# Keeping a weight tile in the array for two sequence blocks: blocks 2 and 3 of the first matmul share each w1 tile

## The chip, the cores and the metric

One core of one Trainium2 chip. The time is the device time of one execution in microseconds; a median over runs is quoted with its range. Most executions of one kernel agree within 0.3%. Every comparison below is between runs in the fast state (a mean granted clock of the tensor engine of at least 0.988 of full speed); the one execution that was not is told of and used for nothing. The experiments ran on four chips, each beside the kernel before on the same chip, and every ratio is to that.

## The reference

```python
B, S, D, F = 1, 2048, 576, 4608          # all bfloat16
def reference(x, w1, b1, w2, b2):
    h = jnp.einsum("bsd,df->bsf", x, w1) + b1
    r = jnp.where(h > 0, h, 0)
    h = r * r                             # squared ReLU
    return jnp.einsum("bsf,fd->bsd", h, w2) + b2
```

## The kernel before

The sequence is cut into four blocks of 512 rows. D = 576 is nine times 64, so the first matmul contracts over 64 rows at a time, and two such matmuls run side by side in the upper and the lower half of the array ("row tiles"). A pair below means two such matmuls, one in each row tile, each streaming 512 columns. The kernel has three parts on the tensor engine:

1. The first matmul, block after block: per block 18 steps; a step makes two tiles of the hidden layer (one per row tile) in two PSUM banks, from 9 pairs. (The first two steps of block 0 are done otherwise while the first inputs arrive, so 70 steps, or 630 pairs, are counted below.) ScalarE then takes each bank out with ReLU and bias, and VectorE squares it.
2. The "64-column part": the last 64 columns of the output, for two blocks at a time, with 128x64 weights from w2.
3. The second matmul proper: per 128 output rows, 36 matmuls of 512 columns with 128x128 weights.

```python
    def a_part(b, j, bk, steps):
        for i in steps:
            for h in range(2):                       # h: upper or lower row tile
                c = ORDER[h][i]
                rows = slice(h * H, (h + 1) * H)
                nc.tensor.matmul(bk[h][:], lhsT=w1h[rows, c, j * P:(j + 1) * P], rhs=xT[b][rows, place(h, c), :],
                                 start=(i == 0), stop=(i == NH - 1))

    def a_step(b, j):
        bk = [bank("ph") for _ in range(2)]          # 8 banks in all, in turn
        a_part(b, j, bk, range(NH))
        for h in range(2):
            evac_h(b, pairs[j][h], bk[h])            # ScalarE: ReLU + bias; VectorE: square
    # ... cut ...
    load_w2(0)
    for b in range(1, NSB):
        for j in (*range(2, NJ), 0, 1):
            a_step(b, j)
            if j == NJ // 2 and b + 1 < NSB:
                finish_xT(b + 1)
        if b == 1:
            load_w2(1)
        if b == 2:
            load_w2(2, 2)                            # the memory of blocks 1 and 2 is free now
    # ... cut ...
    for pr in range(NSB // 2):                       # the 64-column part
        pc = bank("pc")
        for ft in range(NFT):
            for h in range(2):
                nc.tensor.matmul(pc[h * H:(h + 1) * H, :], lhsT=w2(ft, DM, D), rhs=hT_of(2 * pr + h, ft),
                                 start=(ft == 0), stop=(ft == NFT - 1))
        # ... cut: ScalarE adds b2, and a DMA transposes ...
```

Every matmul instruction is compiled into a weight load and a matmul. The transposed x of blocks 0 to 2 lies in memory that w2 takes over later, so a piece of w2 can be loaded only when the block that lay there has been used.

## Time and profile before

| | |
|---|---|
| time, median of the first 3 runs | 290.27 us (290.25 to 290.72) |
| span in the profile | 288.7 us |
| tensor engine (PE) busy | 284.9 us, 99% |
| weight loads (PEld) busy | 133.7 us, 46% |
| chain of waits | 98% PE |

The first two parts of the page: busy time with its share of the span and the number of instructions, and the busy tenths in 40 equal slices. PE is the tensor engine's matmuls, PEld its weight loads, DVE VectorE, ACT ScalarE, POOL GpSimd. PEclk is the granted clock in tenths of full speed (9 is 90% or more).

```profile
PE 284.9 (99%) x2067; PEld 133.7 (46%) x2078; DVE 79.5 (28%) x196; ACT 95.6 (33%) x153; POOL 1.5 (1%) x8
...
PEld 5544444444444444444445444444444444444454
...
PEclk9999999999999999999999999999999999999999
```

A busy PE says little of its pace, because matmuls are pipelined: each is recorded as 376 ns long, and several overlap. The pace is read from the chain of waits in order of time (start, length, what; `ph`, `pc` and `po` are the PSUM tiles of the three parts, and "issue" is time in which PE waited for nothing that the profile shows):

```profile
9.78 135.97 PE ph L213 x1260
145.75 15.66 PE pc L315 x144
161.41 0.32 PE po L329
...
285.97 0.29 DVE o_sb L331
```

The first matmul's 1260 matmuls are 630 pairs in 135.97 us, 215.8 ns a pair. The Trainium skill, "TensorE: Matmul & The Clock Gate", Part 2 (Step-by-step, phases on the wall clock), gives 512 columns at 2.4 GHz as 213 ns plus a fixed 2.5 ns or so, measured at 215.7 ns. This trace agrees.

The groups of instructions (line, engine, operation, shapes, count; busy us and mean ns of one; idle time before them and what ended it):

```profile
L213 PE MATMUL ph<-w_sb,w1h 64*128 64x512 bf16 x936 | 101.2, 376 | 0.0
L213 PEld LDWEIGHTS <-w1h 64*128 64x128 bf16 x1260 | 61.3, 94 | 74.6
...
L213 PE MATMUL ph<-xT,w1h 64*128 64x512 bf16 x324 | 35.1, 376 | 0.0
```

The last column of the matmul lines is 0.0 us of idle time before them. The load line has 74.6 us of idle time, which costs nothing, since loads are not what the others wait for. (How the busy time divides among two groups that overlap is arbitrary.)

### The profile page before, as it was taken

To read this page: it belongs to the slowest core of one execution; us is meant where nothing else is said; L and a number is where in the kernel's file an instruction comes from. 1 tells how busy PE (TensorE), PEld (TensorE's weight loads), DVE (VectorE), ACT (ScalarE), POOL (GpSimd) and SP (SyncE) were. 2 spreads that over 40 slices of the span, in tenths; PEclk is the share of its full clock that TensorE was granted. 3 is DMA by queue.
4 is the path that set the end of the run, shared out by engine and by line. 5 is a ranking of instruction groups with operands and counts; after the bars stand their busy time and mean duration, and the time that the engine had idled before them with its cause. 6 is when DMAs were issued, how large, how long until landed. Compare 5 with 4: busy or idle time off the path is not lost.

```text
span 288.7 us, 4818 instructions
## 1 busy us (share of the span) xinstructions
PE 284.9 (99%) x2067; PEld 133.7 (46%) x2078; DVE 79.5 (28%) x196; ACT 95.6 (33%) x153; POOL 1.5 (1%) x8
## 2 busy tenths in 40 slices
PE   9999999999999999999999999999999999999996
PEld 5544444444444444444445444444444444444454
DVE  1644454444445444444420011111100111111111
ACT  3666666766666676666620000000000000000000
POOL 2000000000000000000000000000000000000000
PEclk9999999999999999999999999999999999999999
DMA  7999999910400004300000100000000000000000
GB/s 200 205 190 204 172 185 208 321 50 2 122 3 0 3 2 142 106 0 2 0 2 19 20 20 20 20 23 5 15 20 23 20 20 20 23 20 22 20 23 20
DMA packets 35381, 18.01 MB, mean 62 GB/s; under 512 B 21652, under 2 KB 35360, under 8 KB 35360
## 3 DMA queue, kind: packets, MB, share of 16 engines
q1 hardware_dynamic: 34752, 17.14, 26.4%
q10 hardware_dynamic: 576, 0.56, 0.6%
q8 instruction: 16, 0.26, 0.4%
q14 instruction: 5, 0.04, 0.0%
q0 software_dynamic: 32, 0.01, 0.0%
HBM read 11.94 MB, written 2.36 MB: 50 GB/s over the span
## 4 chain that ended last, share of the span: by engine, by line
PE 98%; DMA 1%; issue 0%; DVE 0%; ACTq 0%
PE ph L213 47%; PE po L329 43%; PE pc L315 5%; PE ph L228 2%; DMA w_sb<-in_x_dram 1%; PE tp L182 1%; PE ph L254 0%; DVE o_sb L331 0%; PE b1T_ps L247 0%; ACTq L353 0%
## 5 line engine op out<-in xcount | busy, mean ns | idle before, releaser
L197 ACT ACTIVATE r<-ph,b1T 128x512 bf16<-128x512 f32 x144 | 91.0, 685 | 48.4 <-PE ph L213 46.4
L213 PE MATMUL ph<-w_sb,w1h 64*128 64x512 bf16 x936 | 101.2, 376 | 0.0
L213 PEld LDWEIGHTS <-w1h 64*128 64x128 bf16 x1260 | 61.3, 94 | 74.6
L329 PE MATMUL po<-w_sb,hT 128*128 128x512 bf16 x423 | 92.9, 379 | 0.5
L329 PEld LDWEIGHTS <-hT 128*128 128x128 bf16 x432 | 42.2, 98 | 51.2 <-issue 0.4
L199 DVE TENSOR_TENSOR hT<-r 128x512 bf16<-128x512 bf16 x108 | 46.0, 426 | 54.7 <-ACT r L197 54.2
L331 DVE TENSOR_TENSOR o_sb<-po,b_bc 128x512 bf16<-128x512 f32 (+2 forms) x17 | 11.2, 660 | 116.7 <-PE po L329 109.7
L213 PE MATMUL ph<-xT,w1h 64*128 64x512 bf16 x324 | 35.1, 376 | 0.0
L329 PE MATMUL po<-w_sb,w1h 128*128 128x512 bf16 (+2 forms) x178 | 31.2, 336 | 0.1
L329 PEld LDWEIGHTS <-w1h 128*128 128x128 bf16 x180 | 16.2, 98 | 15.3
L199 DVE TENSOR_TENSOR w1h<-r 128x512 bf16<-128x512 bf16 x36 | 15.3, 426 | 19.6 <-ACT r L197 19.5
L315 PE MATMUL pc<-hT,w_sb 128*64 128x512 bf16 x108 | 15.7, 379 | 0.0
L315 PEld LDWEIGHTS <-w_sb 128*64 128x64 bf16 x144 | 8.1, 110 | 7.6 <-issue 0.4
L315 PE MATMUL pc<-w1h,w_sb 128*64 128x512 bf16 x36 | 7.9, 379 | 0.0
L317 ACT ACTIVATE oc<-pc,b2T 128x512 bf16<-128x512 f32 x2 | 1.4, 687 | 13.7 <-PE pc L315 13.7
L325 DVE COPY o_sb<-oc 128x64 bf16<-128x64 bf16 x16 | 2.8, 172 | 9.3 <-DMA oc<-oc 9.3
L228 PE MATMUL ph<-w_sb 128*128 128x256 bf16 x32 | 5.3, 313 | 0.0
L228 PEld LDWEIGHTS <-w_sb 128*128 128x128 bf16 x32 | 3.4, 115 | 0.6
L175 DVE COPY w_sb<-tp 128x256 bf16<-128x256 bf16 x5 | 1.5, 292 | 5.9 <-PE tp L182 5.9
L182 PE MATMUL tp<-ident,w_sb 128*128 128x128 bf16 x20 | 2.7, 264 | 0.1
L169 PE MATMUL wps<-one 128*128 128x512 bf16 x5 | 2.3, 628 | 0.4 <-DVE one L144 0.4
L182 PEld LDWEIGHTS <-w_sb 128*128 128x128 bf16 x20 | 1.9, 118 | 1.4 <-DMA w_sb<-in_x_dram 1.2
(27 smaller groups left out, 10.7 us busy)
## 6 DMA issues: line engine op xcount, KB each, us to landing
w_sb<-in_w_dram SPq DMA_DIRECT2D x2, 1728.0 KB, 8.7
w1h<-in_w_dram SPq DMA_DIRECT2D x8, 288.0 KB, 5.9
out_dram<-o_sb SPq DMA_DIRECT2D x15, 144.0 KB, 1.8
w1h<-in_w_dram SPq DMA_DIRECT2D x12, 144.0 KB, 3.7
w_sb<-in_w_dram SPq DMA_DIRECT2D x2, 864.0 KB, 7.2
w1h<-in_w_dram SPq DMA_DIRECT2D x2, 576.0 KB, 11.2
w_sb<-in_x_dram SPq DMA_DIRECT2D x2, 144.0 KB, 3.4
w_sb<-in_x_dram ACTq DMA_DIRECT2D x2, 144.0 KB, 3.5
```

The lines of the kernel that those rows point to most:

```text
L169: nc.tensor.matmul(wps[:], lhsT=ones[:, 0:P], rhs=ones[:], start=(i == 0), stop=(i == NWARM - 1))
L175: nc.vector.tensor_copy(out=dst, in_=src)
L182: nc.tensor.transpose(tp[:, i * P:(i + 1) * P], xs[:, 2 * half + i, d0:d0 + P], ident[:])
L197: nc.scalar.activation(out=r[:], in_=bk[:], func=ACT.Relu, bias=b1T[:, ft:ft + 1], scale=1.0)
L199: nc.vector.tensor_tensor(out=hT_of(b, ft), in0=r3, in1=r3, op=ALU.mult)
L213: nc.tensor.matmul(bk[h][:], lhsT=w1h[rows, c, j * P:(j + 1) * P], rhs=xT[b][rows, place(h, c), :], start=(i == 0), stop=(i == NH - 1))
L228: nc.tensor.matmul(bk0[q][:, cols], lhsT=qn[:, c, q * P:(q + 1) * P], rhs=xT[0][:, c, cols], start=(half == 0 and c == 0), stop=False, ski ...
L315: nc.tensor.matmul(pc[h * H:(h + 1) * H, :], lhsT=w2(ft, DM, D), rhs=hT_of(2 * pr + h, ft), start=(ft == 0), stop=(ft == NFT - 1))
L317: nc.scalar.activation(out=oc[:, pr, :], in_=pc[:], func=ACT.Identity, bias=b2T[:], scale=1.0)
L325: nc.vector.tensor_copy(out=o_sb[:, DM:D], in_=o_tr[pr][:, jj, h * H:(h + 1) * H])
L329: nc.tensor.matmul(po[:, 0:e - a], lhsT=hT_of(b, ft)[:, jj, :], rhs=w2(ft, a, e), start=(ft == 0), stop=(ft == NFT - 1))
L331: nc.vector.tensor_tensor(out=o_sb[:, a:e], in0=po[:, 0:e - a], in1=b2_bc[:, a:e], op=ALU.add)
```

## The change

The intent: use each w1 tile, once loaded, for two blocks. Blocks 2 and 3 go through the first matmul together, in four banks per step, and a pass over the finished program removes the loads that would load what the array already holds: in a step's round the order is load, matmul of block 2 (upper), load, matmul of block 2 (lower), then both matmuls of block 3 without loads. Because blocks 2 and 3 now end together, the last two pieces of w2 can be loaded only after them, and so the 64-column part is reordered to want those pieces last.

```diff
+    def keep_weights(nc):
+        # ... cut: walk the PE instructions; `held` is what each array tile holds
+            if tile in held and held[tile][0] == what and n - held[tile][1] < 2 * 4 and not (i.has_wait() or i.has_update()):
+                drop.append(i)
+                continue
+            held[tile] = (what, n)
+        for i in drop:
+            block.instructions.remove(i)
+    nc.at_finalize(keep_weights)
...
+    def a_step_pair(bs, j):
+        bk = [[bank("ph") for _ in range(2)] for b in bs]
+        for i in range(NH):
+            for b, k in zip(bs, bk):
+                a_part(b, j, k, (i,))
+        for b, k in zip(bs, bk):
+            for h in range(2):
+                evac_h(b, pairs[j][h], k[h])
...
-    for b in range(1, NSB):
-        for j in (*range(2, NJ), 0, 1):
-            a_step(b, j)
-            ... (finish_xT and load_w2 as shown above)
+    for j in (*range(2, NJ), 0, 1):
+        a_step(1, j)
+        if j == NJ // 2:
+            finish_xT(2)
+        if j == NJ // 2 + 3:
+            finish_xT(3)
+    load_w2(1)
+    for j in (*range(2, NJ), 0, 1):
+        a_step_pair((2, 3), j)
+    load_w2(2, 2)
...
+    pcs = [bank("pc") for _ in range(NSB // 2)]
+    part = 2 * W2CH
+    for fts in ((*range(2 * part, NFT), *range(part)), range(part, 2 * part)):
+        for pr in range(NSB // 2):
+            for ft in fts:
+                for h in range(2):
+                    nc.tensor.matmul(pcs[pr][h * H:(h + 1) * H, :], lhsT=w2(ft, DM, D), rhs=hT_of(2 * pr + h, ft),
+                                     start=(ft == 2 * part), stop=(ft == 2 * part - 1))
```

More of the change, by code (lines that the diff above doesn't have):

```diff
@@ L158 @@
     nc.at_finalize(warm_at_barrier)
+    def keep_weights(nc):
+        block = nc.main_func.blocks[1]
+        held, n, drop = {}, 0, []
+        for i in block.instructions:
+            if i.engine != mybir.EngineType.PE:
+                continue
+            n += 1
+            if not isinstance(i, mybir.InstLdweights):
+                continue
+            tile, what = (tuple(i.tile_position), tuple(i.tile_size)), repr(i.ins)
+            if tile[1] != (H, P):
+                held.clear()
+                continue
+            if tile in held and held[tile][0] == what and n - held[tile][1] < 2 * 4 and not (i.has_wait() or i.has_update()):
+                drop.append(i)
+                continue
+            held[tile] = (what, n)
+        for i in drop:
+            block.instructions.remove(i)
+        print("dropped", len(drop))
+    nc.at_finalize(keep_weights)
     ident = const.tile([P, P], BF16, name="ident")
@@ L296 @@
     load_w2(0)
-    for b in range(1, NSB):
-        for j in (*range(2, NJ), 0, 1):
-            a_step(b, j)
-            if j == NJ // 2 and b + 1 < NSB:
-                finish_xT(b + 1)
-        if b == 1:
-            load_w2(1)
-        if b == 2:
-            load_w2(2, 2)
+    for j in (*range(2, NJ), 0, 1):
[8 more added lines that the diff above has]
+    load_w2(2, 2)
     nc.vector.tensor_copy(out=b2T[:], in_=b2_last[:])
@@ L310 @@
     o_tr = []
-    for pr in range(NSB // 2):
-        pc = bank("pc")
-        for ft in range(NFT):
-            for h in range(2):
-                nc.tensor.matmul(pc[h * H:(h + 1) * H, :], lhsT=w2(ft, DM, D), rhs=hT_of(2 * pr + h, ft),
-                                 start=(ft == 0), stop=(ft == NFT - 1))
+    pcs = [bank("pc") for _ in range(NSB // 2)]
[6 more added lines that the diff above has]
+                                     start=(ft == 2 * part), stop=(ft == 2 * part - 1))
+    for pr, pc in enumerate(pcs):
         nc.scalar.activation(out=oc[:, pr, :], in_=pc[:], func=ACT.Identity, bias=b2T[:], scale=1.0)
```

## The prediction

> **What bounds the kernel now.** The tensor engine, by streaming. The page gives PE 284.9 us busy of 288.7, at full granted clock in every slice; the chain of waits is 98% PE. Busy PE is no proof of peak pace, so I take the pace from the chain: the first matmul (1260 matmuls in two concurrent 64-row tiles) takes 135.97 us, which is 630 pairs at 215.8 ns. In the third part (128x128 weights) 36 matmuls take 7.77 us, again 215.8 ns. The Trainium skill, "TensorE: Matmul & The Clock Gate", Part 2 (phases on the wall clock), gives about 216 ns (215.7 measured) back to back for 512 columns. The trace agrees: both phases already run at the stream's pace, with a weight load before every matmul.
>
> **What the change removes.** In blocks 2 and 3 the load before each of block 3's matmuls: 2 x 18 x 9 = 324 of the 1260, at 94 ns each (groups of instructions), 30 us end to end, about 16 us of "PEld busy" (61.3 us x 324/1260). The weight-load row is busy only 45% of this phase; the loads of both row tiles fit into the 216 ns of the pair before. The same page (Part 2, step 1) says that the next weights load while the present matmul runs, and the groups show no PE idle time before these matmuls (0.0 us). So the removed work is off the critical path: a pair stays at 215.8 ns with or without loads. At best an unloaded pair drops to the bare 512 columns at 2.4 GHz (213.3 ns): 162 pairs x 2.5 ns = 0.4 us, an estimate from that page's clock.
>
> **What it moves.**
> - Evictions come four at a time. In the timeline two ACT evictions take 1.27 us, so four take about 2.6. The step lasts 9 x 2 x 0.216 = 3.88 us, and the other four banks carry the next step. Slack about 1.1 us; no PE wait. VectorE (4 x 0.43 us) follows inside it.
> - The last two w2 chunks (1.7 MB) load only after the paired phase, at about 145.9 us instead of 110.9. There the transfer ran from about 112 to 117.7 us (windows of DMA share); the median to landing of such loads is 8.7 us. So it lands at 153 to 155. The reordered 64-column part does 96 matmuls first, 10.4 us at its measured 108 ns, until about 156. Slack 1 to 3 us; probably no wait.
> - The output transpose of the first pair starts about 5 us later (159 rather than 154), lands at about 162, and is first needed behind an accumulation that ends at about 169. No effect.
> - One VectorE copy pair of 0.6 us moves into block 1, where VectorE is under half busy.
>
> **Predicted time.** 290.2 us, range 289.5 to 291.5. Faster by over 2%: 1%; within 2%: 95%; slower by over 2%: 4%.
>
> **What would show it right or wrong.** Weight loads of the first matmul fall from 1260 to about 936 and PEld busy from 133.7 to about 118 us, while PE busy and span stay. The first matmul should still take 136 us in the chain; a shorter stretch would mean that loads did cost time. PE waiting for a DMA in the 64-column part (about 156 us), or for ACT every 3.9 us in the paired phase, would show a moved cost.
>
> **What would make it wrong.** Matmuls without a load between them may not keep the pace in two row tiles (the trace before has none, so this is untested): each 10 ns lost per unloaded pair is 1.6 us. Or the late w2 load takes over 10.4 us and stalls PE by the excess.

## The result, and the profile after

| | before | after |
|---|---|---|
| median of 4 runs each | 290.26 us (289.88 to 290.72) | 290.53 us (289.69 to 290.63) |
| ratio | | 1.0002, 95% interval 0.9979 to 1.0026 |
| span in the profile | 288.7 us | 288.8 us |
| weight loads, all parts | 2078, 133.7 us busy | 1754, 117.9 us busy |
| PE busy | 284.9 us | 284.9 us |

Ratios are the mean time of one kernel's fast runs over that of the other's of the same rounds, so not quite the ratio of the medians.

The page's first two parts of the changed kernel:

```profile
PE 284.9 (99%) x2067; PEld 117.9 (41%) x1754; DVE 79.3 (27%) x196; ACT 93.5 (32%) x153; POOL 1.5 (1%) x8
...
PEld 5544444444322222222245444444444444444454
...
PEclk9999999999999999999999999999999999999999
```

The load row falls from 4 to 2 tenths between slices 11 and 20, which is the paired phase. The chain of waits in order of time does not move:

```profile
9.91 135.97 PE ph L237 x1260
145.88 15.66 PE pc L351 x144
```

135.97 us and 15.66 us, to the last digit what they were. Both start 0.13 us later, mostly because the first input landed 0.11 us later (an accident of the start). The groups:

```profile
L237 PE MATMUL ph<-w_sb,w1h 64*128 64x512 bf16 x936 | 127.5, 376 | 0.0
...
L237 PEld LDWEIGHTS <-w1h 64*128 64x128 bf16 x936 | 45.6, 94 | 90.2 <-issue 53.8
...
L237 PE MATMUL ph<-xT,w1h 64*128 64x512 bf16 x324 | 61.5, 376 | 0.0
```

324 loads are gone, and their busy time has become idle time of the load row (74.6 to 90.2 us). The matmuls waited 0.0 us before and wait 0.0 us now.

In a stretch of the timeline of the changed kernel (start, length, engine, what, count, idle before) one round of a paired step is visible:

```profile
103.20 0.38 PE L237 MATMUL ph<-xT,w1h 64*128 64x512 bf16 x2
103.20 0.10 PEld L237 LDWEIGHTS <-w1h 64*128 64x128 bf16 x2 [0.33 <-issue]
103.42 0.38 PE L237 MATMUL ph<-w_sb,w1h 64*128 64x512 bf16 x2
103.63 0.38 PE L237 MATMUL ph<-xT,w1h 64*128 64x512 bf16 x2
103.64 0.10 PEld L237 LDWEIGHTS <-w1h 64*128 64x128 bf16 x2 [0.34 <-issue]
103.85 0.38 PE L237 MATMUL ph<-w_sb,w1h 64*128 64x512 bf16 x2
```

`w_sb` marks block 2, `xT` block 3. A pair of matmuls starts every 0.21 to 0.22 us whether or not a pair of loads stands before it. The loads for the next round start as block 3's pair starts (103.20) and are over after 0.10 us, half-way through that pair's stream.

### The profile page after: what moved, and what is told of

Read it like the earlier page. It is cut to its first block, busy times and chain, and to the rows that moved or that the text cites. A ratio compares the mean times of both kernels' runs of the same rounds, so it can differ in the third digit from the quotient of the medians.

```text
span 288.8 us, 4495 instructions
## 1 busy us (share of the span) xinstructions
PE 284.9 (99%) x2067; PEld 117.9 (41%) x1754; DVE 79.3 (27%) x196; ACT 93.5 (32%) x153; POOL 1.5 (1%) x8
## 4 chain that ended last, share of the span: by engine, by line
PE 98%; DMA 1%; issue 0%; DVE 0%; ACTq 0%
PE ph L237 47%; PE po L366 43%; PE pc L351 5%; PE ph L261 2%; DMA w_sb<-in_x_dram 1%; PE tp L206 1%; PE ph L287 0%; DVE o_sb L368 0%; PE b1T_ps L280 0%; ACTq L390 0%
## 5 line engine op out<-in xcount | busy, mean ns | idle before, releaser
L237 PE MATMUL ph<-w_sb,w1h 64*128 64x512 bf16 x936 | 127.5, 376 | 0.0
L221 ACT ACTIVATE r<-ph,b1T 128x512 bf16<-128x512 f32 x144 | 88.9, 686 | 51.4 <-PE ph L237 49.5
L237 PEld LDWEIGHTS <-w1h 64*128 64x128 bf16 x936 | 45.6, 94 | 90.2 <-issue 53.8
L237 PE MATMUL ph<-xT,w1h 64*128 64x512 bf16 x324 | 61.5, 376 | 0.0
L261 PEld LDWEIGHTS <-w_sb 128*128 128x128 bf16 x32 | 3.4, 116 | 0.6
L197 ACT COPY w_sb<-tp 128x256 bf16<-128x256 bf16 x5 | 1.8, 374 | 2.4 <-PE tp L206 2.3
```

What stands on the lines that cost most here:

```text
L197: nc.scalar.copy(out=dst, in_=src)
L221: nc.scalar.activation(out=r[:], in_=bk[:], func=ACT.Relu, bias=b1T[:, ft:ft + 1], scale=1.0)
L261: nc.tensor.matmul(bk0[q][:, cols], lhsT=qn[:, c, q * P:(q + 1) * P], rhs=xT[0][:, c, cols], start=(half == 0 and c == 0), stop=False, ski ...
```

## The experiments

The theory (H): the stream of 512 columns sets the pace; the loads were hidden behind it, and the moved work fits into slack, so neither gain nor loss. Rivals: loads did cost time, and the pairing or the late w2 load gave the gain back (B); or the fixed 2.5 ns above 213.3 ns belong to the weight swap and would go with the loads (S).

### Is a gain hidden by a loss? The change without its removal

`after_again` is the changed kernel once more on the same chip. `loads_kept` has all of the change except the removal:

```diff
-    nc.at_finalize(keep_weights)
```

Expected of `after_again`:

> The changed kernel as it is, on the same chip as the next two, so that they can be compared. Every theory: within 0.3% of the kernel before (290.3 us), as its first four runs were.

Expected of `loads_kept`:

> The changed kernel with the removal switched off: blocks 2 and 3 are still paired in four banks, the w2 load is still late, the 64-column part still reordered, but all 1260 weight loads stand. Theory H (the loads were hidden behind the stream, removing them gives nothing, and the moves cost nothing): 290.3 us, within 0.3% of the changed kernel; the first matmul still takes 136.0 us in the chain; PEld busy back to about 133.7 us. Rival B (removing the loads did save time, and the pairing or the moved load took it back): slower than the changed kernel by what was saved, above 291.5 us; if a quarter of the 30 us of removed load time had counted, 298.

Measured: `after_again` 290.17 us (289.73 to 290.64, 6 runs), ratio to before 0.9999 (0.9983 to 1.0015). `loads_kept` 290.23 us (290.05 to 290.43, 6 runs), ratio 0.9999 with the same interval. The chain and the load group of `loads_kept`:

```profile
9.77 135.97 PE ph L236 x1260
145.74 15.66 PE pc L350 x144
```

```profile
L236 PEld LDWEIGHTS <-w1h 64*128 64x128 bf16 x1260 | 61.4, 94 | 74.6
```

All 1260 loads are back, and the first matmul takes the same 135.97 us. So the removal gives nothing and the pairing takes nothing, each on its own. Rival B falls.

### No loads at all

The kernel before, with nearly all loads of all three parts removed and nothing moved (the result is wrong):

```diff
+    def no_loads(nc):      # keep the first load of each array tile in each part, remove the rest
+        ...
+    nc.at_finalize(no_loads)
```

> The kernel before, wrong result on purpose: of the loads of the first matmul, the 64-column part and the third part only the first of each array tile in each part is kept; over 1900 loads go, nothing is moved. Theory H (512 streamed columns set the pace, 215.8 ns, loads or not): 290.3 us, at least 289.3; 36 matmuls of the third part still take 7.77 us, 1260 of the first 136 us. Rival S (the 2.5 ns above the bare 213.3 ns of 512 columns belong to the weight swap): 213.3 ns a pair everywhere, about 3.2 us less, 287.1. Rival B (loads cost time in the kernel before, and only the pairing hid the gain): the first matmul falls well under 134 us.

The first try gave 289.85 to 290.39 us in five runs, ratio 0.9993 (0.9977 to 1.0009), and 508 us in the profiled one. That execution had a granted clock of 0.56 from about 6.2 us on; it explains nothing here. The kernel was run again for a trace at full clock.

> The kernel without loads once more, for a trace at full clock: the profiled run of the first try took 508 us at a granted clock of 0.56, its five other runs 289.9 to 290.4. Theory H: 36 matmuls of the third part 7.77 us, the first matmul's 1260 in 136 us. Rival S (the 2.5 ns go with the loads): 7.68 us and 134.4 us. If the low clock belongs to this kernel, it comes again in some of the runs; if it was an accident of that run, not.

Measured: 290.24 us (290.03 to 290.51, 4 runs), ratio 1.0001 (0.9986 to 1.0016); the low clock did not come back. 1990 of 2078 loads are gone. The chain:

```profile
9.64 135.97 PE ph L234 x1260
145.62 15.66 PE pc L336 x144
161.28 124.53 PE po L350 x612
```

Without loads the pairs take the same 215.8 ns, the 64-column part the same 15.66 us, and the third part 124.5 us as before (161.41 to 285.94 there). Rival S falls too: whatever the 2.5 ns are, they do not go with the loads. This bounds every plan of this kind in this kernel: removing every load in it is worth nothing that these runs can show. Why one execution in ten of this kernel was granted a low clock stays open.

### What the moves hang on: the late w2 load

The changed kernel with the reorder of the 64-column part undone, so that the late pieces are wanted after 12 row tiles instead of at the end:

```diff
-    for fts in ((*range(2 * part, NFT), *range(part)), range(part, 2 * part)):
+    for fts in ((*range(part), *range(part, 2 * part)), range(2 * part, NFT)):
```

(`start` and `stop` follow the new order.)

> The changed kernel with the order of the 64-column part undone: the w2 chunks that are loaded last (rows tiles 12 to 23) are wanted after 12 row tiles, at about 148.4 us, instead of after 48 half passes at 156.2. Reading of the late load (issued at 146, landed between 153 and 154.5, so free only thanks to the reorder): PE waits 5 to 6 us for the DMA in this part, and the kernel takes 295 to 296.5 us. If the load lands earlier than I read, less.

Measured: 297.84 us (297.51 to 298.33, 4 runs), ratio 1.0263 (1.0243 to 1.0284): 7.6 us, more than the 5 to 6 expected. The waits and three stretches of the trace (columns: us, then busy us and count of PE, PEld, DVE, ACT, POOL, then the granted clock, DMA share, GB/s):

```profile
PE pc L351 <- DMA w_sb<-in_w_dram: 4.9, 1, 4.9
```

```profile
148.25:153.30 5.05, 0.12 (x4) 0.01 (x2) 0.16 (x2) 0.00 (x0) 0.00 (x0) 0.90 0.85 292
153.30:159.20 5.90, 5.90 (x28) 2.47 (x30) 0.00 (x0) 0.00 (x0) 0.00 (x0) 0.51 0.00 0
159.20:169.30 10.10, 10.10 (x95) 5.03 (x92) 0.00 (x0) 0.69 (x1) 0.00 (x0) 1.00 0.07 14
```

PE waited 4.9 us for the DMA, near what was read: the load was wanted at 148.4 us, and PE went on at 153.3. What the expectation lacked is the clock. PE then ran at half clock for 5.9 us, which is some 2.9 us of work lost; together 7.8 us against 7.6 measured. The Trainium skill, "TensorE: Matmul & The Clock Gate", Part 1 (What's actually happening), says that an idle window of about 3.4 us sends the array to half rate and about as much sustained work brings it back. The trace agrees in kind: 5 us idle, then a clock of 0.51; but the full clock came back only after 5.9 us of work, longer than the page's figure. So the late load is free only because the reorder puts 48 pairs in front of it: the pieces are wanted at 156.3 us in the changed kernel (145.88 and 96 matmuls of 108.75 ns), and PE could go on at 153.3 in this run, 3 us of slack.

### What the moves hang on: the other four banks

The changed kernel with all pairs in the same four banks:

```diff
+    pair_banks = []
     def a_step_pair(bs, j):
-        bk = [[bank("ph") for _ in range(2)] for b in bs]
+        if not pair_banks:
+            pair_banks.extend([bank("ph") for _ in range(2)] for b in bs)
+        bk = pair_banks
```

> The changed kernel, with the pairs of blocks 2 and 3 all in the same four banks, so that the next step cannot start while the four evictions run. Reading of the evictions (the last of four ends about 2.6 us after the last matmul, hidden behind the next step only because that has the other four banks): PE waits for ACT between the 18 steps, some 2.2 us each, 17 times, so about 37 us more, 328 us, and more if the clock falls in the gaps. Rival B' (the banks do not matter because evictions are done sooner): under 300 us.

Measured: 325.48 us (325.40 to 325.81, 4 runs), ratio 1.1217 (1.1200 to 1.1233), 35 us more. A period of its chain of waits, and the four evictions in the timeline, in this run and then in the changed kernel:

```profile
82.50 3.43 PE ph L237 x30
...
88.42 1.67 PE ph L237 x13
```

```profile
85.95 2.42 ACT L221 ACTIVATE r<-ph,b1T 128x512 bf16<-128x512 f32 x4 [3.50 <-PE ph L237]
102.97 2.42 ACT L221 ACTIVATE r<-ph,b1T 128x512 bf16<-128x512 f32 x4 [1.47 <-PE ph L237]
```

A step now takes 88.42 - 82.50 = 5.92 us instead of 9 x 2 x 0.2158 = 3.88, and 17 times the difference is 35 us. The four evictions take 2.42 us in both; in the changed kernel ScalarE has 1.47 us to spare before them. So the evictions would cost 2.0 us a step if the next step did not have four other banks; in the changed kernel they are fully hidden.

### When does removing loads pay? Shorter streams

To find where a load stops being free, the matmuls of blocks 2 and 3 in the changed kernel were cut into pieces of 128 and of 64 columns, once with a load before every piece and once with the repeated loads removed:

```diff
-                a_part(b, j, k, (i,))
+                for s in range(4):                  # or 8
+                    cols = slice(s * SB // 4, (s + 1) * SB // 4)
+                    for h in range(2):
+                        ... the same matmul on k[h][:, cols] and xT[b][..., cols],
+                            start=(i == 0 and s == 0), stop=(i == NH - 1)
```

The stream alone is estimated in these expectations from the clock of 2.4 GHz and the fixed 2.5 ns a matmul of the page cited above ("TensorE: Matmul & The Clock Gate", Part 2): 55.8 ns for 128 columns, 26.7 + 2.5 ns for 64. That a load might need 53 ns, its 128 columns at the same clock, is an assumption that the runs test.

> The changed kernel with each matmul of blocks 2 and 3 cut into four of 128 columns, and all loads kept: four times the loads for the same columns, a load (94 ns from start to end) before each stream of 53 to 56 ns. If a tile takes one load after another at 94 ns: at least 4 x 94 = 376 ns instead of 216 for each of 324 pairs, 52 us more, 342 us. If loads overlap one another (in the last row block 36 matmuls of 128 columns with a load each took about 61 ns each): some 4 x 61 = 244 ns, 9 us more, 299 us. Theory H in either case: where a load no longer fits behind the stream before it, it costs time.

> The same cut into 128 columns, but with all repeated loads removed: one load for eight matmuls of a tile. Theory H: 4 x 55.8 = 223 ns for a pair, 324 x 7 ns = 2.4 us above the changed kernel, about 293 us, so that here the same removal pays by the difference to the run with loads (6 to 50 us). If the issue of matmuls binds instead (eight short matmuls in 216 ns), it is slower than 295 us and the removal pays less.

> The changed kernel with the matmuls of blocks 2 and 3 cut into eight of 64 columns, all loads kept: eight times the loads. In four pieces a tile took a load and a matmul every 56 ns, so a load that the trace shows as 94 ns long can start at least that often. Theory H, refined (a load hides as long as a new one can start within the stream before it): if a load needs its 128 columns at the full clock, about 53 ns, 8 x 53 = 427 ns for a pair instead of 216, 68 us more, about 359 us. Rival: loads can start every 29 ns, and nothing is paid but the fixed part of the matmuls, about 296 us, the same as without loads.

> The same cut into 64 columns with the repeated loads removed: one load for sixteen matmuls of a tile. Stream alone: 8 x (26.7 + 2.5) = 233 ns for a pair, 5.7 us above the changed kernel, about 296 us. If the issue of matmuls binds (sixteen in 233 ns), slower[...]; then load removal is worth less than the stream alone says.

The length of the paired phase is the difference of starts in the chain of waits; instructions are matmuls and loads of PE in that phase.

| run | median us (range) | ratio to before | paired phase | PE instructions in it | ns each |
|---|---|---|---|---|---|
| changed kernel | 290.17 | 0.9999 | 69.9 us (324 x 215.8 ns) | 972 | 72 |
| split4_kept | 294.68 (294.38 to 295.16) | 1.0152 (1.0134 to 1.0170) | 74.87 us | 5,184 | 14.4 |
| split4_dropped | 292.87 (292.82 to 293.03) | 1.0092 (1.0077 to 1.0107) | 72.36 us | 2,916 | 24.8 |
| split8_kept | 366.31 (365.07 to 366.50) | 1.2598 (1.2573 to 1.2624) | 145.86 us | 10,368 | 14.1 |
| split8_dropped | 298.95 (297.90 to 299.80) | 1.0299 (1.0276 to 1.0322) | 78.15 us | 5,508 | 14.2 |

`split4_dropped` is the stream alone, 223.3 ns for four pieces, as expected. That also says where the 2.5 ns go: three more matmuls per pair cost 223.3 - 215.8 = 7.5 ns, 2.5 ns each, so they come with every matmul, loaded or not. `split4_kept` has four times the loads in the same time and loses only 2.5 us more, of which 1.17 us are three gaps in the chain: a load recorded as 94 ns does not keep the next one waiting for 94 ns. Both of my expectations for it (342 and 299 us) were too high.

In `split8_kept` the expected 359 us (a load every 53 ns) was nearly met, at 366, but by luck: the trace shows another cause. Its chain of waits, and then a group of loads and two of matmuls in its timeline:

```profile
101.76 1.69 issue
103.44 2.04 PE ph L248 x128
105.49 1.41 issue
106.90 2.04 PE ph L248 x128
```

```profile
103.45 1.93 PEld L248 LDWEIGHTS <-w1h 64*128 64x128 bf16 x128 [1.80 <-issue]
```

```profile
103.73 0.41 PE L248 MATMUL ph<-xT,w1h 64*128 64x64 bf16 x16
103.97 0.41 PE L248 MATMUL ph<-w_sb,w1h 64*128 64x64 bf16 x16
```

PE works in bursts of 128 matmuls and 128 loads. Inside a burst 128 matmuls take 2.04 us, which is 16 in about 0.23 us once the burst runs, the estimated pace of the bare stream (8 x (26.7 + 2.5) = 233 ns): even a load in each row tile every 29 ns is hidden. Then nothing happens for 1.4 to 1.7 us. (An earlier gap, of 3.1 us, was followed by a burst at half clock that took 3.26 us; that is 1.2 us of the 145.86.) The Trainium skill, "Runtime: NRT & Kernel Launch" (Instruction fetch mechanics), says that an engine's instructions are fetched in 16 KiB blocks of 256. The trace agrees: the DMA queue of kind "instruction" moved 51 packets and 0.84 MB here, 16,384 bytes each, and 51 x 256 is 13,056 of PE's 13,228 recorded instructions (6,614 matmuls and as many loads):

```profile
q8 instruction: 51, 0.84, 0.9%
```

against 15 packets and 0.25 MB in the changed kernel, where PE has 3,832 instructions (2,078 matmuls and 1,754 loads in the trace of `after_again`, which misses no record). The new theory (I): PE's instructions come at about 14 ns each, and the phase takes the longer of its stream and its instructions. To tell it from a limit on a tile's loads (L), `split8_half` removes the repeated loads of the lower row tile only:

```diff
-            if tile in held and ...:
+            if tile[0][0] == H and tile in held and ...:
```

> Eight pieces of 64 columns, repeated loads removed for the lower row tile only; the upper tile keeps a load before each of its matmuls, eight in 233 ns. Theory I (in the run with all loads kept, the array took a load every 29 ns without delay inside a burst, and the loss is instruction supply: bursts of 128 matmuls and 128 loads, then a gap of 1.4 to 1.7 us; 10,368 instructions in 145.9 us, 14.1 ns each): now 7,776 instructions less 162 x 2 at most, about 324 x 24 x 14.1 ns = 109 us for the paired phase instead of 146, total about 330 us, gaps after every 256 instructions still. Theory L (a tile's loads need about 53 ns each): the upper tile still takes as many loads as before and holds the pair up as before, 360 us or more.

Measured: 331.97 us (331.29 to 332.19, 4 runs), ratio 1.1431 (1.1405 to 1.1456). The exact count is 5,184 matmuls and 2,754 loads, 7,938 instructions (my count in the expectation was loose); the paired phase takes 186.59 - 76.23 = 110.4 us, 13.9 ns each. The chain:

```profile
137.98 0.85 issue
138.83 2.61 PE ph L250 x168
141.44 1.12 issue
142.56 2.62 PE ph L250 x167
145.18 0.83 issue
```

The upper row tile takes as many loads as before, and the phase is 35 us shorter. The gaps are still there, shorter and after more matmuls (about 168 with some 84 loads, again about 256 instructions; a few records are missing from the trace). Theory L falls, and theory I holds within 2%.

The start times of the instruction queue's packets in the packed traces show the supply directly. In the paired phase (less 3 us at each end) one packet of 256 instructions follows another every 3.58 us on average in `split8_kept`, 3.54 in `split8_half`, 3.60 in `split8_dropped` and 3.67 in `split4_kept`, which is 13.8 to 14.3 ns an instruction, although a packet itself takes about 1.05 us. Where PE needs fewer instructions the packets come as needed: every 6.3 us in `split4_dropped`, every 18.7 us in the changed kernel. What spaces the fetches 3.6 us apart is not shown. Theory I also explains the two runs near the balance: `split4_kept` has 5,184 x 14 ns = 73 us of instructions against 72.4 us of stream and took 74.9, and `split8_dropped` has 77 us of instructions against 324 x 233 ns = 75.5 us of stream and took 78.2. The kernel before is far from it, with 4 instructions per pair of 215.8 ns, 54 ns each.

## Why the prediction was right

The time (290.2 against 290.53, and 290.17 in the repeat), the range and the class held, and the mechanism was tested part by part.

- "The removed work is off the critical path: a pair stays at 215.8 ns with or without loads." Shown: 135.97 us for the first matmul before, after, with loads kept, and with nearly no loads.
- "At best an unloaded pair drops to 213.3 ns": it does not. The run without loads kept 215.8 ns.
- Weight loads 1260 to 936, PEld busy to about 118 us, PE busy unchanged: measured 936, 117.9 us and 284.9 us.
- Evictions: "four take about 2.6 us, slack about 1.1, no PE wait". Four take 2.42 us, ScalarE has 1.47 us to spare, and no PE wait appears. That the other four banks are what hides them is shown by the 35 us of the four-bank run.
- The late w2 load: predicted to land at 153 to 155 and to be wanted at about 156. In the run that waited for it, PE went on at 153.3.
- The output transpose of the first pair of blocks was to land at about 162; the copy that waits for it started at 162.2 us, and PE did not notice.
- One term under "what would make it wrong" was mis-sized, though it did not come up: a late load "stalls PE by the excess". With the reorder undone, 4.9 us of waiting cost 7.6 us, because the idle engine lost its clock for another 5.9 us.
- "30 us end to end" for the removed loads was a count of recorded durations and not of array time. The recorded 94 ns is the length of one load's record, not the interval at which loads can start: in bursts a tile took a load every 29 ns. The prediction's conclusion did not need that number, but a reader who took 94 ns for the price of a load would expect far too much from removing loads, as my expectations for the 128-column runs did.

## What to carry to other kernels

Before removing weight loads, compare the pace of the matmuls (from the chain of waits, not from busy time) with the bare stream of their columns; if they agree, the loads are hidden and their removal frees only a row of the profile that nobody waits for. Reuse of loaded weights paid here where streams were short, and what it saved was instructions, not loading time, so count instructions per stream. No run here found a stream so short that loading itself cost time. When a change moves work into slack, test the slack alone, and count for a stall of the tensor engine of several microseconds the slower clock after it as well.

## What the Trainium skill lacked or had wrong

- "TensorE: Matmul & The Clock Gate", LDWEIGHTS (loading the stationary operand), gives a load's time as columns over 1.2 (107 ns for 128); the trace has 94 ns for 64x128 loads, and 110 ns for the 128x64 loads of the 64-column part, which have half the columns. The page has no measured interval between the starts of bf16 loads, which is what matters (under Weight-path perf modes it has one in theory, for fp8): one every 29 ns in each of two row tiles was hidden in bursts of the 64-column run.
- The same page has, under Back-to-back issue gap, about 131 ns a matmul as the sustained pace of load and matmul at 512 columns; here the third part, with a load of the whole array before every matmul, took 215.8 ns a matmul (7.77 us for 36), and the first matmul 215.8 ns a pair of row tiles, with loads, with half of them in blocks 2 and 3, and with nearly none. That is the figure that the page gives for the isolated gap (about 216).
- "Runtime: NRT & Kernel Launch", Instruction fetch mechanics, says that instruction fetch is hidden because the sequencer issues more slowly than fetching fills. On PE with short matmuls it was not: with 32 instructions per 233 ns of stream the phase took 145.86 us where its stream needs 75.5, at about 14 ns an instruction, with gaps of 1.4 to 1.7 us after every 256, and one 16 KiB packet of instructions arriving every 3.58 us.
- No page tells of one execution in ten of a kernel without weight loads at a granted clock of 0.56 from about 6.2 us on (508 us); these runs do not settle why.
